# Loading V of a head pair as two transfers of 64 rows, in place of one transfer per head with an outer dimension of two

## The chip, the cores and the metric

One core of a Trainium2 chip. The metric is the device time of one execution in microseconds. The experiments were taken in two sessions on two chips: e1 to e4 on one, where the kernel before took 3283.57 us, and e5, e6 and e8 on the other, where it took 3284.61 us.

## The reference

Plain attention with a softmax over all keys, in bf16:

```python
B, H, Sq, Sk, D = 16, 32, 192, 1024, 128      # q, k, v: normal * 0.05, bf16
scores = jnp.einsum("bhqd,bhkd->bhqk", q, k) * D ** -0.5
p = softmax(scores, axis=-1)
return jnp.einsum("bhqk,bhkd->bhqd", p, v)
```

There are 512 heads, which the kernel treats as 256 pairs. The scores are tiny, so the softmax is nearly uniform. The comparison with the reference cannot see whether V's rows are paired with the right keys within a head.

## The kernel before

For each pair, K, Q and V come from memory by DMA, all issued from one queue (the sync engine, SP). The profile counts 16 DMA engines for the core, and the trace records each transfer as packets. Data land in SBUF, where the tiles of this kernel that take K, Q and V have 128 partitions (rows); the tensor engine's results go to tiles in PSUM. DVE is the vector engine, ACT the scalar engine, POOL the GpSimd engine; PEld is the weight loading of PE. The tensor engine (PE) transposes K through PSUM (L569), DVE copies that back to SBUF (L656), PE forms the scores (L590), ACT takes the exponential (L707), POOL copies V into a buffer with a column of ones (L549), and PE multiplies by V (L608). K has 4 buffers, V has 10.

```python
def load_k(p):
    if p >= R:                                   # R = 4
        e.wait_ge(s_tr, 2 * (p - R) + 2)
    e.dma_start(kn[:, p % R, :],
        kf[2*p:2*p+2].rearrange("x (m s) d -> (x m) (s d)", s=2*T),   # T = 8
    ).then_inc(s_kn[p % R], 16)
# ... load_q: a transposing DMA ...
def load_v(p):
    if p >= NVS:                                 # NVS = 10
        e.wait_ge(s_pv, p - NVS + 1)
    for x in range(2):
        e.dma_start(vs[:, p % NVS, x, :],
            vf[2*p + x].rearrange("(m w t) d -> w m (t d)", w=2, t=T),
        ).then_inc(s_v[p % NVS], 16)
# ... the order of issue, at pair n of the main loop ...
    load_k(n + R); load_q(n + R)
    load_v(n - 2 + NVS)
    # every fourth pair: store(...)
```

The layout `w m` is not arbitrary. K is loaded with 16 consecutive keys per partition, so the score rows on partition 64w + m belong to keys 16m + 8w to 16m + 8w + 7, and V has to follow. PE does, for each pair ("step"), twice: a QK group of 20 matmuls, a transpose group of 16, a PV half of 24:

```python
for t in range(T):
    # ...
        for w in range(2):
            ins = pe.matmul(S[64*w: 64*w+64, c0: c0 + (j1-j0)*64],
                kt[:, p % R, 8*w + t, 64*x: 64*x+64], mv,
                start=True, stop=True, tile_position=(0, 64*w))
```

## Time and profile before

| | before |
|---|---|
| time | 3282.99 us (median of 3) |
| PE busy | 45% |
| mean DMA busy | about 0.3 |
| clock granted to PE | 0.713 |

The first three fences are of the kernel before. First, the page: engine, busy us, share of the span, instructions; then the busy tenths and the clock in 40 slices; then DMA issues with the time from issue to landing.

```profile
span 3280.7 us, 67883 instructions
...
PE 1471.8 (45%) x30722; PEld 1423.9 (43%) x30722; DVE 546.6 (17%) x1031; ACT 744.2 (23%) x513; POOL 267.4 (8%) x263
...
PEclk6677767777677767777767777676677776767667
DMA  2333333333323333333333233333333333333333
...
f_kn<-in_k_dram SPq DMA_DIRECT2D x256, 512.0 KB, 14.5
```

No engine is busy even half of the time and DMA is at about 0.3. Both are averages, over all time and over all 16 DMA engines, and both mislead. The view of waits (engine, line, what it waited for: us in total, times, longest) shows who stands still:

```profile
POOL f_vp L549 <- PE f_o L608: 2943.5, 252, 66.0
...
PE f_k L569 <- PEq L558: 1783.0, 251, 81.2
...
POOL f_vp L549 <- DMA f_vs<-in_v_dram: 49.1, 4, 17.3
```

PE is idle for 1783 us ahead of the K transposes, in 251 stretches, one per pair. "PEq L558" is PE's own queue taking a semaphore; for the first transpose of a pair that semaphore is K's. POOL waits for V only four times: V is not late after the start, K almost always is. The windows view (stretch, busy us and count of PE, PEld, DVE, ACT and POOL, clock, DMA share, GB/s) shows what the DMA does meanwhile:

```profile
core 0: us, PE busy (x) PEld busy (x) DVE busy (x) ACT busy (x) POOL busy (x), PEclk, DMA share, GB/s
60.00:100.00 40.00, 0.00 (x0) 0.00 (x0) 0.00 (x0) 0.00 (x0) 0.00 (x0) 0.50 0.13 50
300.00:600.00 300.00, 139.03 (x2880) 134.57 (x2880) 50.94 (x96) 69.65 (x48) 25.00 (x24) 0.72 0.32 99
```

From 60 to 100 us nothing computes, and DMA share is 0.13 = 2/16. I read this as two DMA engines at 25 GB/s each and fourteen idle. The packet records of the trace say the same of the middle of the run: for 64% of the time exactly two packets are in flight. The timeline of one pair in the middle:

```profile
1007.44 4.77 SPq L479 DMA_DIRECT2D f_kn<-in_k_dram  x1
1010.35 0.85 PEld L569 LDWEIGHTS f_k<-f_ident,f_kn 128*64 128x64 bf16 x16 [7.22 <-issue]
1010.38 1.06 PE L569 MATMUL f_k<-f_ident,f_kn 128*64 128x128 bf16 x16 [7.04 <-PEq L558]
1011.10 1.40 PEld L608 LDWEIGHTS f_o<-f_vp,f_pt 128*64 128x64 bf16 x24
...
1012.27 2.68 SPq L487 DMA_TRANSPOSE f_qt<-in_q_dram  x1
```

The transposes at 1010.38 start after 7.04 us of idle. The single K issue before them took 4.77 us; the shortest one in this trace took 0.41, which I read as a full queue ahead of it.

I took the cause from the shape of the transfer: V's source has `w` = 2 outermost, and 0.13 is the share of two engines. That the outermost dimension sets the number of engines was my assumption; the trace of this kernel alone does not show it.

### The profile page before, as it was taken

To read this page: it belongs to the slowest core of one execution; us is meant where nothing else is said; L and a number is where in the kernel's file an instruction comes from. 1 tells how busy PE (TensorE), PEld (TensorE's weight loads), DVE (VectorE), ACT (ScalarE), POOL (GpSimd) and SP (SyncE) were. 2 spreads that over 40 slices of the span, in tenths; PEclk is the share of its full clock that TensorE was granted. 3 is DMA by queue.
4 is the path that set the end of the run, shared out by engine and by line. 5 is a ranking of instruction groups with operands and counts; after the bars stand their busy time and mean duration, and the time that the engine had idled before them with its cause. 6 is when DMAs were issued, how large, how long until landed. Compare 5 with 4: busy or idle time off the path is not lost. (4 is left out here: it accounts for less than half of the span.)

```text
span 3280.7 us, 67883 instructions
## 1 busy us (share of the span) xinstructions
PE 1471.8 (45%) x30722; PEld 1423.9 (43%) x30722; DVE 546.6 (17%) x1031; ACT 744.2 (23%) x513; POOL 267.4 (8%) x263
## 2 busy tenths in 40 slices
PE   1344444444444444444444444444444444444454
PEld 1344444444444344444444444444444444444444
DVE  0111111111111111111111111111111111111112
ACT  1122222222222222222222222222222222222222
POOL 0000000000000000000000000000000000000000
PEclk6677767777677767777767777676677776767667
DMA  2333333333323333333333233333333333333333
GB/s 74 91 101 94 102 97 99 97 103 93 103 93 103 97 96 100 98 98 97 99 98 103 93 103 93 103 97 99 97 97 99 99 97 97 104 93 103 93 103 89
DMA packets 243763, 319.35 MB, mean 97 GB/s; under 512 B 112640, under 2 KB 145408, under 8 KB 243712
## 3 DMA queue, kind: packets, MB, share of 16 engines
q1 hardware_dynamic: 243712, 318.82, 31.6%
q14 instruction: 38, 0.31, 0.2%
q8 instruction: 13, 0.21, 0.1%
HBM read 268.44 MB, written 25.17 MB: 89 GB/s over the span
## 5 line engine op out<-in xcount | busy, mean ns | idle before, releaser
L707 ACT ACTIVATE f_pt<-f_s 128x1536 bf16<-128x1536 f32 x512 | 742.9, 1451 | 2522.3 <-PE f_s L590 2519.5
L569 PE MATMUL f_k<-f_ident,f_kn 128*64 128x128 bf16 x8192 | 501.5, 292 | 1783.3 <-PEq L558 1783.0
L569 PEld LDWEIGHTS f_k<-f_ident,f_kn 128*64 128x64 bf16 x8192 | 432.5, 159 | 1830.1 <-issue 1830.1
L656 DVE COPY f_kt<-f_k 128x1024 bf16<-128x1024 bf16 x512 | 354.3, 692 | 2561.5 <-PE f_k L569 2561.4
L608 PE MATMUL f_o<-f_vp,f_pt 128*64 128x129 bf16 x12288 | 660.0, 279 | 2.2 <-PEq L558 2.2
L608 PEld LDWEIGHTS f_o<-f_vp,f_pt 128*64 128x64 bf16 x12288 | 600.0, 152 | 2.7 <-issue 2.7
L590 PE MATMUL f_s<-f_qt,f_kt 128*64 128x192 bf16 (+2 forms) x10240 | 589.9, 276 | 14.4 <-issue 14.4
L549 POOL COPY f_vp<-f_vs 128x1024 uint32<-128x1024 uint32 x256 | 266.5, 1041 | 2992.6 <-PE f_o L608 2943.5
L590 PEld LDWEIGHTS f_s<-f_qt,f_kt 128*64 128x64 bf16 x10240 | 496.6, 140 | 14.8 <-issue 14.8
L671 DVE TENSOR_TENSOR f_ob<-f_o,f_rinv 128x384 bf16<-128x384 f32 x256 | 142.7, 558 | 8.9
L667 DVE RECIPROCAL f_rinv<-f_o 128x3 f32<-128x3 f32 x256 | 46.4, 181 | 155.9 <-PE f_o L608 155.8
L707 ACT ACT_TABLE_LOAD x1 | 1.3, 1283 | 0.8 <-PEq L733 0.8
L680 DVE TENSOR_TENSOR f_chk<-f_chk,f_rinv 128x750 f32<-128x750 f32 (+1 forms) x2 | 1.1, 560 | 0.1
L681 DVE TENSOR_REDUCE f_bad<-f_chk 128x1 bf16<-128x750 f32 (+1 forms) x2 | 1.1, 556 | 0.1
L679 DVE TENSOR_SCALAR f_chk<-f_rinv 128x750 f32<-128x750 f32 (+1 forms) x2 | 1.0, 508 | 0.0
L640 PE MATMUL f_o<-f_bad,f_ones 128*1 128x1 bf16 x1 | 0.2, 164 | 1.4 <-DVEq L696 1.4
L640 PEld LDWEIGHTS f_o<-f_bad,f_ones 128*1 128x1 bf16 x1 | 0.1, 79 | 1.6 <-DVEq L696 1.6
L541 POOL TENSOR_SCALAR_AFFINE_SELECT f_ident<-f_ones 128x128 bf16<-128x128 bf16 x1 | 0.3, 292 | 0.1
L539 POOL MEMSET f_ones<- 128x128 bf16 x1 | 0.2, 204 | 0.3 <-POOLq L733 0.3
L544 POOL MEMSET f_vp<- 128x128 bf16 x1 | 0.2, 212 | 0.0
L698 DVE CAST redo<-f_o 1x1 int32<-1x1 f32 x1 | 0.1, 147 | 0.3 <-PE f_o L641 0.3
L641 PE MATMUL f_o<-f_bad,f_ones 128*1 128x1 bf16 x1 | 0.2, 163 | 0.0
(5 smaller groups left out, 0.5 us busy)
## 6 DMA issues: line engine op xcount, KB each, us to landing
f_kn<-in_k_dram SPq DMA_DIRECT2D x256, 512.0 KB, 14.5
f_vs<-in_v_dram SPq DMA_DIRECT2D x512, 256.0 KB
out_dram<-f_ob SPq DMA_DIRECT2D x64, 384.0 KB, 15.1
f_qt<-in_q_dram SPq DMA_TRANSPOSE x256, 10.7
```

The lines of the kernel that those rows point to most:

```text
L549: gp.tensor_copy(vp[:, p % R, :, 0:D].bitcast(U32), vs[:, p % NVS, :, :].rearrange("p x (t d) -> p (x t) d", d=D).bitcast(U32),).then_inc( ...
L569: ins = pe.transpose(k_ps[64 * z: 64 * z + 64, t * 128: t * 128 + 128], kn[:, p % R, c0: c0 + 64], ident[:], tile_position=(0, 64 * z))
L590: ins = pe.matmul(S[64 * w: 64 * w + 64, c0: c0 + (j1 - j0) * 64], kt[:, p % R, 8 * w + t, 64 * x: 64 * x + 64], mv, start=True, stop=True ...
L608: ins = pe.matmul(o_ps[64 * x: 64 * x + 64, j * 129: j * 129 + 129], pt[:, (2 * p + x) % NP, t * SQ + j * 64: t * SQ + j * 64 + 64], vp[:, ...
L640: pe.matmul(o_ps[0:1, 0:1], ones[:, 0:1], bad[:, 0:1], start=True, stop=False)
L656: dve.tensor_copy(kt[:, p % R, 8 * y: 8 * y + 8, :], k_ps[:].rearrange("d (t c) -> d t c", c=128),).then_inc(s_ev, 1)
L667: dve.reciprocal(ri, O[:, :, 128]).then_inc(s_rc, 1)
L671: dve.tensor_tensor(ob[:, so, a, :].rearrange("p (j d) -> p j d", j=3), O[:, :, 0:128], ri.unsqueeze(2).to_broadcast([128, 3, D]), ALU.mul ...
L679: done(dve.tensor_scalar(chk[:, lo:hi], rinv[:, lo:hi], 1.0 / RS_HI, 1.0 / RS_LO, ALU.max, ALU.min))
L680: done(dve.tensor_tensor(chk[:, lo:hi], chk[:, lo:hi], rinv[:, lo:hi], ALU.not_equal))
L681: done(dve.tensor_reduce(bad[:, i: i + 1], chk[:, lo:hi], mybir.AxisListType.X, ALU.max))
L707: act.activation(pt[:, h % NP, :], s_ps[h % 2][:], ACT_FN.Exp, scale=scale).then_inc(s_exp, 1)
```

## The change

The intent: keep bytes, layout and the number of transfers, but make the outermost dimension 64, in the expectation that V is then spread over 16 engines.

```diff
-                    for x in range(2):
+                    for w in range(2):
                         e.dma_start(
-                            vs[:, p % NVS, x, :],
-                            vf[2 * p + x].rearrange("(m w t) d -> w m (t d)", w=2, t=T),
+                            vs[64 * w: 64 * w + 64, p % NVS, :, :],
+                            vf[2 * p:2 * p + 2].rearrange("x (m w t) d -> w m x (t d)", w=2, t=T)[w],
                         ).then_inc(s_v[p % NVS], 16)
```

## The prediction

> **What bounds the kernel now.** Not the tensor engine: the busy table has it at 45%, and the view of waits shows 1783.0 us of idle before the K transposes in 251 stretches, 7 us in each of the 256 pairs, ended by the tensor queue's wait for the K load. DMA is busy only 31.6% on average, but in the packet records of 1500 to 1513 us exactly two packets are in flight for 63% of the time, and from 60 to 100 us (view of windows) no engine computes while DMA share is 0.13, two sixteenths, at 50 GB/s. The V source has an outer dimension of two, so it runs on two DMA engines ([...] the 0.13 agrees). Per pair, on such an engine, from median packet times: V 128 packets x 84 ns = 10.75 us, K 8 x 159 = 1.27, Q 24 x 18 = 0.43, stores 8 x 36 = 0.29; sum 12.75, x 256 = 3263 of 3281 us. These two engines are the bound. V is early (POOL waits for it 4 times only); K pays, since two of its sixteen shares queue behind V.
>
> **What the change does.** Bytes, packet sizes and number of transfers stay. 64 rows outermost give 16 engines, so per engine V becomes 16 x 84 = 1.34 us and DMA needs at least 3.3 us a pair. But each transfer writes only 64 partitions. [...]
>
> **The next limits.** Tensor: the clock is now low in 58% of its recorded time. In the high state, weight load starts give 0.473 us for a K transpose group, 0.700 for a PV half, 0.644 for a QK group; two of each is 3.63 us a pair, against 6.56 in the low one. Vector normalisation may add 0.1. ACT is 2 x 1.451 = 2.9, POOL 1.04, DVE 2.1. SP issue, from the shortest issues (K 0.41, Q 1.18, V 2 x 0.51), is 2.6; longer ones now are full queues. Tensor gives 3.7 x 256 = 950, plus about 30 us of start and end, 980; [...] All of the removed 8 us lies on the critical path.
>
> **Prediction:** 1085 us, range 980 to 1185. Faster by over 2%: 0.985; within 2%: 0.01; slower: 0.005.
>
> **Signs.** DMA's busy share rises from 0.32 to 0.8 or more, at about 290 GB/s; the hole at 60 to 100 us goes; granted clock rises from 0.71 to near 1; tensor busy falls from 1472 to about 950 us; the 1783 us of idle falls below 250; K lands in 4 to 6 us, not 14.5. [...] 85 to 100 ns mean a tensor limit (near 990).
>
> **What would make it wrong.** V not spread over 16 engines; SP issue dearer for the 64-row form, or SP's in-order waits shortening K's lead; the tensor clock staying low despite dense work; memory unable to feed 16 engines at 300 GB/s.

The sum came to 4.1 us a pair, so 4.1 x 256 + 30 = 1080 us, put at 1085: a choice of mine between the 3.7 us of the tensor engine, 980 us in all, and the pace that I expected if V were slowed in full, which lay at the upper end of the range. The last sign, 85 to 100 ns, is that of a V packet.

## The result

| | before | after |
|---|---|---|
| time, median (4 runs each) | 3282.39 us | 1199.99 us (1199.16 to 1202.05) |
| ratio | | 0.3657 (0.3651 to 0.3663) |
| PE busy | 1471.8 us, 45% | 995.0 us, 83% |
| granted clock | 0.713 | 0.988 |

A ratio is the mean time of one kernel's fast runs over that of the other's fast runs of the same rounds, so it is not quite the ratio of the medians. The time lies 15 us above the top of the stated range.

The same views of the kernel after. The page:

```profile
span 1197.7 us, 67883 instructions
...
PE 995.0 (83%) x30722; PEld 947.9 (79%) x30722; DVE 546.4 (46%) x1031; ACT 744.1 (62%) x513; POOL 268.1 (22%) x263
...
PEclk9799999999999999999999999999999999999999
DMA  9999999999999999999999999999999999999991
...
f_kn<-in_k_dram SPq DMA_DIRECT2D x256, 512.0 KB, 9.9
```

The waits:

```profile
POOL f_vp L549 <- PE f_o L608: 890.3, 252, 18.6
...
PE f_k L569 <- PEq L558: 186.0, 245, 17.6
POOL f_vp L549 <- DMA f_vs<-in_v_dram: 18.6, 4, 9.3
```

The windows:

```profile
core 0: us, PE busy (x) PEld busy (x) DVE busy (x) ACT busy (x) POOL busy (x), PEclk, DMA share, GB/s
60.00:100.00 40.00, 35.99 (x1159) 35.23 (x1155) 19.79 (x37) 28.41 (x20) 9.41 (x9) 1.00 1.07 256
300.00:600.00 300.00, 257.57 (x7976) 245.48 (x7972) 141.07 (x267) 192.43 (x133) 69.95 (x67) 0.99 1.08 276
600.00:900.00 300.00, 257.02 (x7994) 244.56 (x7990) 140.94 (x266) 193.60 (x134) 68.89 (x66) 1.00 1.08 276
```

All 16 DMA engines now work all the time (the share is over 1, because more than 16 packets overlap: in the packet records 16 to 22 are in flight nearly all the time), PE's clock is 0.99 to 1.00 in these windows, and the idle time before the K transposes is a tenth of what it was. But it is not gone: 186 us in 245 stretches, and K takes 9.9 us to land. I read this as DMA still being the limit, now with all of its engines; the share alone would not show it, since the tensor-limited runs below have 1.06. The number of engines can be counted too: packets of 4 bytes, which I take for one end mark per engine and transfer, number 14336 before and 21504 after, 14 more for each of the 512 V transfers. The other packets show where the time goes. Worked out from them (each value is the packets' total time over 16 engines and 256 pairs):

```
                 packets per    before:            after:
                 engine, pair*  mean ns, us/pair   mean ns, us/pair
V   2048 B            16          88     1.41       153     2.46
K   4096 B             8         232     1.86       199     1.59
Q    256 B            24          19     0.46        18     0.43
store 768 B            8          36     0.29        43     0.35
sum                                      4.02               4.83
* averaged over 16 engines; before, V's 256 packets of a pair ran on two
```

A V packet took 84 ns at the median before and takes 159 ns now. The mean pace between the 40th and 240th pair, taken from POOL's copies, is 4.52 us a pair after and 12.68 before.

### The profile page after: what moved, and what is told of

Its sections match the earlier page's. It is cut to its first block, busy times and chain, and to the rows that moved or that the text cites. A ratio compares the mean times of both kernels' runs of the same rounds, so it can differ in the third digit from the quotient of the medians.

```text
span 1197.7 us, 67883 instructions
## 1 busy us (share of the span) xinstructions
PE 995.0 (83%) x30722; PEld 947.9 (79%) x30722; DVE 546.4 (46%) x1031; ACT 744.1 (62%) x513; POOL 268.1 (22%) x263
## 5 line engine op out<-in xcount | busy, mean ns | idle before, releaser
L569 PE MATMUL f_k<-f_ident,f_kn 128*64 128x128 bf16 x8192 | 331.2, 221 | 186.2 <-PEq L558 186.0
L608 PE MATMUL f_o<-f_vp,f_pt 128*64 128x129 bf16 x12288 | 459.3, 221 | 2.2 <-PEq L558 2.2
L569 PEld LDWEIGHTS f_k<-f_ident,f_kn 128*64 128x64 bf16 x8192 | 276.1, 110 | 232.1 <-issue 232.0
L590 PE MATMUL f_s<-f_qt,f_kt 128*64 128x192 bf16 (+2 forms) x10240 | 444.4, 231 | 5.2 <-issue 5.2
L608 PEld LDWEIGHTS f_o<-f_vp,f_pt 128*64 128x64 bf16 x12288 | 395.8, 110 | 2.7 <-issue 2.7
L590 PEld LDWEIGHTS f_s<-f_qt,f_kt 128*64 128x64 bf16 x10240 | 360.4, 111 | 5.7 <-issue 5.7
```

What stands on the lines that cost most here:

```text
L569: ins = pe.transpose(k_ps[64 * z: 64 * z + 64, t * 128: t * 128 + 128], kn[:, p % R, c0: c0 + 64], ident[:], tile_position=(0, 64 * z))
L590: ins = pe.matmul(S[64 * w: 64 * w + 64, c0: c0 + (j1 - j0) * 64], kt[:, p % R, 8 * w + t, 64 * x: 64 * x + 64], mv, start=True, stop=True ...
L608: ins = pe.matmul(o_ps[64 * x: 64 * x + 64, j * 129: j * 129 + 129], pt[:, (2 * p + x) % NP, t * SQ + j * 64: t * SQ + j * 64 + 64], vp[:, ...
```

## The experiments

**What to explain.** That two DMA engines were the bound before, and why V packets take 1.7 times as long after (153 ns on average against 88). Three theories for the second:

- *Destination.* The cost comes from which SBUF partitions a transfer writes: 0 to 63 or 64 to 127, in place of all 128. The expectations call this the port theory and gave a mechanism for it, which no trace here shows.
- *Source.* Each new transfer reads every other 2 KB of memory, and might meet only half of it.
- *Total.* Sixteen engines cannot get more than about 275 GB/s here.

Source and destination were therefore varied one at a time. Five of these kernels pair V's rows with the wrong keys. In three of them (e1, e3 and e4) each row stays in its head, and the comparison with the reference still passed, because the softmax is nearly uniform; that is no proof of a right kernel. In e2 and e8 it fails.

### Contiguous source, still 64 partitions (e1_contig64)

```diff
-    vf[2*p:2*p+2].rearrange("x (m w t) d -> w m x (t d)", w=2, t=T)[w],
+    vf[2*p:2*p+2].rearrange("x (w m t) d -> w m x (t d)", w=2, t=T)[w],
```

> V rows taken contiguously from memory (result wrong on purpose), still 64 partitions per transfer, 16 DMA engines. Port theory [...]: no change, 1190 to 1210 us, V packets stay near 153 ns mean. Source theory (each transfer of the change reads only every other 2 KB of memory and so hits only part of it): V packets fall to about 90 ns and the time to 980 to 1020 us. Total-bandwidth theory (16 engines cannot get more than about 275 GB/s): 1200 us.

Measured: 1198.52 us (1197.09 to 1202.27, 4 runs), V packets 152.7 ns mean. The window, columns as above, is that of the changed kernel:

```profile
300.00:600.00 300.00, 255.87 (x7959) 243.39 (x7956) 140.05 (x265) 192.55 (x134) 68.80 (x66) 1.00 1.08 276
```

This is what the destination theory said, and the total theory too; the source theory falls.

### The change's source, but 128 partitions (e2_strided128)

```diff
-    vs[64*w: 64*w+64, p % NVS, :, :],
-    vf[2*p:2*p+2].rearrange("x (m w t) d -> w m x (t d)", w=2, t=T)[w],
+    vs[:, p % NVS, w, :],
+    vf[2*p:2*p+2].rearrange("x (m w t) d -> w x m (t d)", w=2, t=T)[w].rearrange("x m e -> (x m) e"),
```

> The same alternating 2 KB rows read from memory as in the changed kernel, but each transfer writes all 128 partitions (result wrong on purpose). Port theory: V packets fall to 85 to 95 ns, K packets back to about 160, time 970 to 1010 us with the tensor engine as the limit. Source theory: V packets stay near 153 ns and the time 1190 to 1210 us. Total-bandwidth theory: 1200 us.

Measured: 982.59 us (979.74 to 983.12), V packets 110 ns mean and 87 median, K packets 170 mean. The windows of this run, columns as above:

```profile
300.00:600.00 300.00, 300.00 (x9826) 300.00 (x9822) 173.64 (x328) 237.35 (x165) 85.25 (x82) 1.00 1.06 341
600.00:900.00 300.00, 300.00 (x9825) 300.00 (x9821) 173.32 (x327) 237.69 (x164) 84.92 (x83) 1.00 1.06 341
```

PE is busy all the time and 341 GB/s flow in place of 276, so the total theory falls too. The wait before the K transposes is down to 16.2 us in the whole run:

```profile
PE f_k L569 <- PEq L558: 16.2, 7, 9.1
```

The V packets were expected at 85 to 95 ns; their mean is higher through a tail (the slowest 1% take over 680 ns), which no longer matters for the time.

### Contiguous source and 128 partitions (e3_contig128)

```diff
-  for w in range(2):
+  for x in range(2):
-    vs[64*w: 64*w+64, p % NVS, :, :],
-    vf[2*p:2*p+2].rearrange("x (m w t) d -> w m x (t d)", w=2, t=T)[w],
+    vs[:, p % NVS, x, :],
+    vf[2*p + x].rearrange("(m t) d -> m (t d)", t=T),
```

> Contiguous source and 128 partitions (result wrong on purpose), one transfer per head. Port theory and source theory both: V packets 85 to 95 ns, 970 to 1010 us. Total-bandwidth theory: 1200 us.

Measured: 982.05 us (981.17 to 983.34), V packets 110 ns. With this the square is complete: 64 partitions 1200 and 1199 us, 128 partitions 983 and 982 us, whatever the source.

### Four engines (e4_four_engines)

```diff
 (of the kernel before)
-    vf[2 * p + x].rearrange("(m w t) d -> w m (t d)", w=2, t=T),
+    vf[2 * p + x].rearrange("(m w t) d -> w m (t d)", w=4, t=T),
```

> The kernel before with the outer dimension 4 in place of 2 (result wrong on purpose). If the outer dimension sets the number of DMA engines, V runs on 4. Without port sharing that is 64 packets x 84 ns + 1.99 us = 7.4 us a pair, 1890 to 1930 us. With port sharing [...] V packets take about 150 ns, 64 x 150 + 2.0 = 11.6 us, about 2970 us, although only about 60 GB/s flow for V. If the engine count was not the bound of the kernel before: 3280 us.

"Port sharing" stands here for V packets slowed to about the 150 ns of the changed kernel.

Measured: 2242.6 us in one run, between the two numbers expected. One digit in the source pattern, with the same bytes, packets and issues, takes 1041 us off the kernel before (3283.57 us in these rounds): the number of engines was its bound. There are 15360 packets of 4 bytes, two more per V transfer than before, as four engines in place of two would leave. Exactly four packets are in flight for 44% of the time. The windows:

```profile
300.00:600.00 300.00, 174.94 (x4159) 168.41 (x4155) 73.44 (x139) 101.51 (x70) 36.45 (x35) 0.83 0.58 144
600.00:900.00 300.00, 169.16 (x4200) 162.64 (x4200) 74.20 (x140) 101.51 (x70) 36.45 (x35) 0.86 0.58 144
```

V packets take 109.7 ns on average; 57% of them took 80 to 90 ns, and a broad second group lies around 140 to 170. So V packets were slowed here too, at only 144 GB/s in all, but not all of them; by what, this run does not show. The account of the two engines before carries over with the measured packet: 64 x 110 = 7.0 us of V a pair and engine, with the 1.99 us expected for the rest 9.0, against a pace of 8.67 us.

### Sixty-four partitions in the middle (e8_middle_64)

If the partitions are the cause and not the 64 rows, another choice of 64 partitions may cost nothing. Partitions 32 to 95 were tried. Both transfers write there, into two buffers; the other partitions of the buffer in use are zeroed once at the start.

```diff
-vs = sb("f_vs", [128, NVS, 2, T * D], BF16)
+vs = sb("f_vs", [128, NVS, 2, 2, T * D], BF16)
-    vs[64*w: 64*w+64, p % NVS, :, :],
+    vs[32:96, p % NVS, w, :, :],
# POOL: two memsets of the other partitions of vs; its copy reads vs[:, p % NVS, 0, :, :]
```

> Still two transfers of 64 partitions, but both write partitions 32 to 95 (two buffers, unwritten partitions zeroed once; result wrong on purpose). Port theory: [...] V packets fall to the 110 ns mean of the 128-partition runs and the steady pace to 3.7 us a pair; total 975 to 1015 us with the zeroing at the start. A theory that any transfer of 64 rows is slow, whichever partitions it writes: V near 153 ns, 1200 us.

Measured: 981.56 us (979.52 to 983.88), V packets 111 ns mean, 87 median. The windows:

```profile
300.00:600.00 300.00, 300.00 (x9823) 300.00 (x9820) 173.35 (x328) 237.33 (x165) 85.73 (x82) 1.00 1.06 341
600.00:900.00 300.00, 300.00 (x9823) 300.00 (x9819) 173.63 (x328) 237.53 (x164) 85.02 (x82) 1.00 1.06 340
```

Same number and size of transfers, same 64 rows, same source as in the changed kernel, other partitions: 218 us less, and the wait before the K transposes is down to 13.5 us. So it is the choice of partitions that costs the time. By what mechanism the partitions act is not shown.

### Upper half from a second queue (e6_second_half_from_act)

The forecast had supposed that V would be slowed only in part. In the changed kernel the two halves follow each other in one queue; here they are issued from two, so that transfers to both halves can be under way at once.

```diff
-  for w in range(2):      # in the sync queue
+  for w in range(1):
# scalar engine: pairs 0 to 3 ahead of its loop, then before the exponential of head 2n
+  act.dma_start(vs[64:128, ...], ...[1]).then_inc(s_v[p % NVS], 16)   # pair n + 4
```

> The changed kernel, with the upper 64 partitions of V issued from the scalar engine's queue, so that each DMA engine has packets for both halves at hand at once; right result. [...] V packets 100 to 130 ns, time 1000 to 1120 us. If the order of the halves in the queue has no part in it: V packets near 153 ns, 1190 to 1210 us. The scalar engine pays about 0.6 us of issue per pair, which its 38% of idle time covers.

The first pair of figures are for the case that the order of the halves in one queue keeps V slow.

Measured: 1187.24 us (1177.65 to 1194.85), 1% less than with one queue (ratio to before 0.3622, 0.3604 to 0.3640, against 0.3657). V packets take 140 ns on average over both queues (160 in the first, 120 in the second), so V eases by a tenth, to 2.24 us a pair; but K packets rise to 207 ns and Q packets to 22, and the DMA share stays at 1.08, at 282 GB/s in place of 276. The result lies between the two expectations and much nearer the second: having the halves in two queues takes a small part of the slowing away, and the order of the halves in the queue is not what mainly keeps it up.

The trace can say whether the engines are in step. The semaphore of a K load is raised 16 times, which I read as once by each engine at the end of its share. In the changed kernel these 16 marks lie within 0.08 us at the median, and within 0.10 us in 90% of the loads, while a half of V keeps an engine busy for 8 x 153 ns = 1.2 us. So, read this way, the engines end a K load in step; in the runs in which V is not slowed like this (e2, e3, e5, e8: V packets at 99 to 111 ns on average) the marks lie just as close (0.08 us). With the second queue the marks spread over 0.30 us at the median, and over up to 0.94 us in 90% of the loads: some drift, and V packets at 140 ns in place of 153. What keeps the engines in step stays open.

### One transfer of 128 partitions, right result (e5_natural_kv)

V can be loaded naturally, 8 consecutive keys per partition, if K is loaded in the same way. Then partition 64w + m of the scores holds keys 8(64w + m) to 8(64w + m) + 7 of head x, and only the index of the stationary operand changes.

```diff
# load_k
-    kn[:, p % R, :],
-    kf[2*p:2*p+2].rearrange("x (m s) d -> (x m) (s d)", s=2*T),
+    kn[:, p % R, :].rearrange("m (x e) -> m x e", x=2),
+    kf[2*p:2*p+2].rearrange("x (m t) d -> m x (t d)", t=T),
# load_v: one transfer, and POOL waits for 16 in place of 32
-    (the two transfers of the change)
+    vs[:, p % NVS, :, :],
+    vf[2*p:2*p+2].rearrange("x (m t) d -> m x (t d)", t=T),
# QK
-    kt[:, p % R, 8*w + t, 64*x: 64*x+64], mv,
+    kt[:, p % R, 8*x + t, 64*w: 64*w+64], mv,
```

> A right version: K and V of a pair each in one transfer of 128 partitions with two 2 KB rows per partition, and the QK product picks its K columns accordingly. Port theory: the two rows per partition do no harm, V packets about 110 ns mean and 86 median as in the two runs with 128 partitions, tensor engine at about 97% busy, 3.66 us a pair, 975 to 990 us. A theory that two rows per partition (not the 64 partitions) slow the packets: V near 150 ns and 1200 us or more, since K now has them too.

Measured: 983.04 us (981.50 to 984.05), ratio to before 0.2991 (0.2986 to 0.2996). The comparison passes; as it can't see the order of keys, the order rests on the derivation: kn[m', x, t] is key 8m' + t of head x, its transpose stands in kt column group 8x + t at column m', the score of it on partition m', and V's row 8m' + t on the same partition. The waits and the windows:

```profile
PE f_k L568 <- PEq L557: 17.1, 7, 9.9
```

```profile
300.00:600.00 300.00, 300.00 (x9823) 300.00 (x9819) 173.32 (x328) 237.03 (x165) 85.43 (x82) 1.00 1.07 339
600.00:900.00 300.00, 300.00 (x9822) 300.00 (x9818) 173.50 (x328) 237.29 (x164) 84.70 (x82) 1.00 1.07 340
```

PE is busy 300 of 300 us. This is the tensor limit at full clock: 3.67 us a pair from POOL's copies, x 256 = 939 us, and the other 43 us of the 982 us span are start and end, in which the first pairs wait for their loads. The 2 KB packets, now K's and V's together, take 99 ns on average and 86 at the median. This version beats both kernels; two rows per partition do no harm.

## Why the prediction was wrong

- **The bound of the kernel before: right.** Two engines, 12.75 us a pair worked out and 12.68 measured; the four-engine run moved it by changing their number. One part of the account does not fit: "two of its sixteen shares queue behind V". Every K load has 16 end marks, one for each engine as I read them (see the second queue). In 25 of the 192 loads before whose marks I could group, the last two come late, by 8.3 us at the median; in 165 of the other 167 all sixteen lie within 0.2 us, some 14 us after the issue. So as a rule the whole K load waited, not two shares of it. Why fourteen less loaded engines did not run ahead stays open.
- **Sixteen engines, a higher clock, the hole gone: right.** DMA share 1.08, clock 0.988, PE busy 995 us (950 forecast), idle before the K transposes 186 us (below 250 forecast). K's landing was forecast at 4 to 6 us and took 9.9, a miss; the runs that write 128 partitions come to what was forecast (5.3 us in e2).
- **The tensor limit: right.** 3.7 us a pair and 980 us in all were forecast; the runs with V packets at 99 to 111 ns show 3.67 (e5) and 982 (e3).
- **The sign of slow V packets: right.** The signs named two outcomes, and slow V packets with a DMA limit, over 1100 us, as one of them; V packets of 153 ns, where they had taken 88, and 1200 us came. The mechanism is not shown.
- **The step that failed:** the 4.1 us a pair, taken in the belief that V would be slowed only in part. The slowing was larger: V packets took 153 ns on average and 159 at the median, and the pace was 4.52. That is (4.52 - 4.1) x 256 = 108 us. V cost 2.46 us a pair against the 1.34 of 84 ns a packet, and K packets suffered as well (1.59 us against 1.27 forecast and 1.36 in the runs with 128 partitions), a term the sum did not have. In packet time the sum was 4.83 us, and packets overlap (share 1.08).
- **A second term was too small:** 30 us for start and end. The span of 1198 us less 256 x 4.52 leaves 41. The range ended at 1185 us, 15 us below the result, and these 11 us are most of that.

No run had shown what half-width transfers cost when the forecast was made: for the full slowing I had a figure that no trace of it had shown, for how far the 16 engines would escape it nothing at all, and I put the middle of the forecast between no slowing and the full one. The four-engine run shows that V packets can be slowed in part (its mean is 110 ns), but not that these 16 engines would be.

## What to carry to other kernels

Average DMA share did not show the bound here: 0.32 hid two engines that were always busy, and 1.08 and 1.06 belonged to one run limited by DMA and one limited by the tensor engine. Look for how many DMA engines are active, and read the outermost dimension of each transfer: 2, 4 and 64 went here with two, four and sixteen engines. After spreading a transfer over 16 engines, ask a second question, which SBUF partitions it writes: transfers to partitions 0 to 63 and 64 to 127 cost some 218 us more here than the same bytes to 32 to 95, or to all 128. In the trace this looked like 2 KB packets at a mean of 153 ns, where they had taken 88, and a DMA share of 1.08 with 276 GB/s flowing, where 341 flowed at 1.06. If a layout forces half-width transfers, look for a layout of the other operand that removes the need; here one index of the K operand did it.
